# One query projection as two units of their own, and a layer norm in two stages ordered by hand

## The chip, the cores and the metric

The kernel runs on 1 core of one Trainium2 chip. The metric is the device time of one execution in microseconds (us), less is better. The engines are named as the profile names them: PE (TensorE matmul), PEld (its weight load), DVE (VectorE), ACT (ScalarE), POOL (GpSimd), SP (SyncE, which only issues transfers here).

## The reference, cut to what matters

```python
x = A_x                                     # (1, 2048, 640), bf16
xn = layernorm(x)
q = (xn @ wq)                               # 32 heads of 192
p = softmax(q k^T / sqrt(192))              # keys and values: 2048 per head
s = (p v) @ wo
g = silu( (silu(xn @ w1) * (xn @ w3)) @ w2 )
return x + s * g
```

Most of the time goes to scores and values of the 32 heads: the last projection, the one for head 31, ends 1825 us into the 2169, and the scores and values of head 31 are still to come. The query projection of a head has 192 columns: 128, and 64 more. The 64 more share a 128-column matmul with 64 columns of w1 or w3, so each head and query block needs two matmul groups of five: one with `wqB` (64 columns of w1 or w3, and 64 of the query) and one with `wq` (the first 128 of the query).

## The kernel before

The kernel's matmuls write to PSUM tiles: one ring of three of 1024 fp32 columns (`ps_st`, tag `st2`), which scores, projections, transposes and the output all use in turn, and one tile (`obank`) for the values. A unit of work is one head and one block of 512 queries: two score groups of four score tiles, each followed by a group of value matmuls, and then the projection of the same block for the next head.

```python
def project(h, qb):
    ...
    ps = ps_st.tile([P, 1024], F32, tag="st2", name="ps")
    for c in range(DC):                                      # line 288: first half
        nc.tensor.matmul(ps[:, 512:1024], lhsT=L["wqB"][:, c, :], rhs=xnT[:, c, qs], ...)
    nc.scalar.copy(out=qAB[:, 1, qs], in_=ps[:, 512:1024])   # line 289
    for c in range(DC):                                      # line 291: second half
        nc.tensor.matmul(ps[:, 0:512], lhsT=L["wq"][:, c, 0:P], rhs=xnT[:, c, qs], ...)
    nc.vector.tensor_copy(out=qAB[:, 0, qs], in_=ps[:, 0:512])
    nc.gpsimd.dma_start(out=qC[0:64, :, qs], in_=qAB[64:P, :, qs])
    nc.gpsimd.dma_start(out=qC[64:P, 0, qs], in_=qAB[0:64, 0, qs])

# scores of one tile read KA, KB, KC (keys) and qAB, qC (queries);
# KC and qC are copies on other partitions, made by DMA from POOL's queue

load_x(0); load_w(0); load_k(0)            # load_k also issues the KC copies
...
load_w(1); load_k(1); load_v(1)            # (cut) loads of head 1
...
layer_norm(0)                              # statistics, rstd on POOL, xn, transposes
project(0, 0)
pending = emit_scores(*stream[0][:3])
layer_norm(1)
project(0, 1)
for n, (h, qb, pairs, first, last) in enumerate(stream):
    pts = pending
    if n + 1 < len(stream):
        pending = emit_scores(*stream[n + 1][:3])
    ...                                    # values of group n into obank
    if h == 0 and first and qb + 2 < NQB:
        layer_norm(qb + 2)
        project(0, qb + 2)
    if not last:
        continue
    ...                                    # DVE: reciprocal, scaling of obank into ostage
    if h + 1 < H:
        project(h + 1, qb)
    ...
```

The traces show the instructions of each engine in the order of this program (in the kernel before, POOL's `rstd` at 33.91 us stands behind the key copies at 31.26 and 33.35). The program names no waits between engines; the framework puts them in.

Of the kernel before, what the change touches and what calls it, by code (L numbers as in the profile page):

```python
# [9 lines left out]
ALU = mybir.AluOpType  # L10
AX = mybir.AxisListType
BF16 = mybir.dt.bfloat16
F32 = mybir.dt.float32
I32 = mybir.dt.int32

P = 128
# [76 lines left out]
def _output_stage(nc, i, oT, g, wo_sb, x2, out2, sb, ps_pool):  # L93

    D = out2.shape[1]
    OC = wo_sb.shape[1]
    xt = sb.tile([P, D], BF16, tag="xt", name="xt")
    nc.gpsimd.dma_start(out=xt[:], in_=x2[i * P:(i + 1) * P, :])
    ps = ps_pool.tile([P, 1024], F32, tag="st2", name="ps_s")
    for k in range(OC):  # L100
        for b, (c0, c1) in enumerate(_column_pieces(D)):
            nc.tensor.matmul(ps[:, b * 512:b * 512 + c1 - c0], lhsT=oT[:, k, :], rhs=wo_sb[:, k, c0:c1],  # L102
                             start=(k == 0), stop=(k == OC - 1))
    tmp = sb.tile([P, D], F32, tag="tmp", name="tmp")
    res = sb.tile([P, D], BF16, tag="res", name="res")
    for b, (c0, c1) in enumerate(_column_pieces(D)):
        nc.vector.scalar_tensor_tensor(out=tmp[:, c0:c1].rearrange("p (a w) -> p a w", w=P),  # L107
                                       in0=ps[:, b * 512:b * 512 + c1 - c0].rearrange("p (a w) -> p a w", w=P),
                                       scalar=0.5, in1=g[:, c0 // P:c1 // P, :], op0=ALU.mult, op1=ALU.mult)
        nc.vector.tensor_tensor(out=res[:, c0:c1], in0=tmp[:, c0:c1], in1=xt[:, c0:c1], op=ALU.add)  # L110
    nc.scalar.dma_start(out=out2[i * P:(i + 1) * P, :], in_=res[:])
# [9 lines left out]
def _kernel_impl(  # L121
# [95 lines left out]
    def load_k(h):  # L217
        kh = A_k_cache[0, h]
        KA = kvp.tile([P, SK], BF16, tag="KA", name="KA")
        nc.sync.dma_start_transpose(out=KA[:], in_=kh[:, 0:P])  # L220
        KB = kvp.tile([P, SK], BF16, tag="KB", name="KB")
        nc.sync.dma_start_transpose(out=KB[:], in_=kh[:, DH - P:DH])  # L222
        KC = kvp.tile([P, HK], BF16, tag="KC", name="KC")
        nc.gpsimd.dma_start(out=KC[64:P, :], in_=KA[0:64, HK:SK])
        nc.gpsimd.dma_start(out=KC[0:64, :], in_=KB[64:P, 0:HK])
        loads.setdefault(h, {}).update(KA=KA, KB=KB, KC=KC)

    def load_v(h):
        vt = vts[h % 2]
        nc.sync.dma_start(out=vt[:, :, 0:DH], in_=A_v_cache[0, h].rearrange("(t p) d -> p t d", p=P))  # L230
        loads.setdefault(h, {}).update(vt=vt)

    load_x(0)
    load_w(0)
    load_k(0)
    for g in range(1, NQB):
        load_x(g)
    load_v(0)
    load_w(1)
    load_k(1)  # L240
    load_v(1)
    mhalf = const.tile([P, 4], F32, name="mhalf")
    nc.vector.memset(mhalf[:], -0.5)
    for vt in vts:
# [4 lines left out]
    while D // nsub > nc.vector.BN_STATS_FMAX or D % nsub != 0:  # L249
        nsub += 1  # L250

    def layer_norm(g):
        mv = lnp.tile([P, 4, nc.vector.BN_AGGR_DIM], F32, tag="mv", name="mv")
        for i in range(4):
            stats = lnp.tile([P, nsub, nc.vector.BN_STATS_DIM], F32, tag="stats", name="stats")
            xr = x_sb[:, 4 * g + i, :].rearrange("p (a f) -> p a f", a=nsub)
            for a in range(nsub):
                nc.vector.bn_stats(out=stats[:, a, :], in_=xr[:, a, :])  # L258
            nc.vector.bn_aggr(out=mv[:, i, :], in_=stats[:])
        ve = lnp.tile([P, 4], F32, tag="ve", name="ve")  # L260
        nc.vector.tensor_scalar(out=ve[:], in0=mv[:, :, 1], scalar1=eps, scalar2=None, op0=ALU.add)
        rstd = lnp.tile([P, 4], F32, tag="rstd", name="rstd")
        nc.gpsimd.tensor_tensor(out=rstd[:], in0=ve[:], in1=mhalf[:], op=ALU.pow)  # L263
        for i2 in range(2):
            pst = ps_st.tile([P, 2, DC, P], BF16, tag="st2", name="pst")
            for k in range(2):
                i = 2 * i2 + k
                xn = lnp.tile([P, D], BF16, tag="xn", name="xn")
                nc.vector.tensor_scalar(out=xn[:], in0=x_sb[:, 4 * g + i, :], scalar1=mv[:, i, 0:1], scalar2=rstd[:, i:i + 1],  # L269
                                        op0=ALU.subtract, op1=ALU.mult)  # L270
                for c in range(DC):
                    nc.tensor.transpose(out=pst[:, k, c, :], in_=xn[:, c * P:(c + 1) * P], identity=ident_bf[:])  # L272
            q0 = (4 * g + 2 * i2) * P
            nc.scalar.copy(out=xnT[:, :, q0:q0 + 2 * P].rearrange("p c (k q) -> p k c q", k=2), in_=pst[:])  # L274
# [1 line left out]

    qtiles = {}

    def project(h, qb):

        L = loads[h]
        if qb == 0:
            qtiles[h] = (qp.tile([P, 2, SQ], BF16, tag="qAB", name="qAB"), qlp.tile([P, 2, SQ], BF16, tag="qC", name="qC"))
        qAB, qC = qtiles[h]
        qs = slice(qb * 512, (qb + 1) * 512)
        ps = ps_st.tile([P, 1024], F32, tag="st2", name="ps")
        for c in range(DC):
            nc.tensor.matmul(ps[:, 512:1024], lhsT=L["wqB"][:, c, :], rhs=xnT[:, c, qs], start=(c == 0), stop=(c == DC - 1))  # L288
        nc.scalar.copy(out=qAB[:, 1, qs], in_=ps[:, 512:1024])  # L289
        for c in range(DC):  # L290
            nc.tensor.matmul(ps[:, 0:512], lhsT=L["wq"][:, c, 0:P], rhs=xnT[:, c, qs], start=(c == 0), stop=(c == DC - 1))  # L291
        nc.vector.tensor_copy(out=qAB[:, 0, qs], in_=ps[:, 0:512])  # L292
        nc.gpsimd.dma_start(out=qC[0:64, :, qs], in_=qAB[64:P, :, qs])  # L293
        nc.gpsimd.dma_start(out=qC[64:P, 0, qs], in_=qAB[0:64, 0, qs])  # L294

    def swiglu(h, qb):

# [42 lines left out]
            pts.append(pT2)  # L340
        return pts

    layer_norm(0)
    project(0, 0)
    pending = emit_scores(*stream[0][:3])
    layer_norm(1)
    project(0, 1)
    obank = None
    ostage = None
    w_all = None  # L350
    for n, (h, qb, pairs, first, last) in enumerate(stream):
        if first and qb == 0:
            if h == H // 2:
                w_all = fw.tile([P, WX], BF16, tag="xw", name="w_all")
                w2_sb = w_all[:, 0:FC * D].rearrange("p (c d) -> p c d", d=D)
                nc.sync.dma_start(out=w2_sb, in_=B_w2.rearrange("(c p) d -> p c d", p=P))
                w1_sb = w3_sb = None
                if FL > 0:
                    o1 = FC * D
                    w1_sb = w_all[:, o1:o1 + DC * FL].rearrange("p (c f) -> p c f", f=FL)  # L360
                    w3_sb = w_all[:, o1 + DC * FL:o1 + 2 * DC * FL].rearrange("p (c f) -> p c f", f=FL)
                    nc.sync.dma_start(out=w1_sb, in_=B_w1[:, FPIG:F].rearrange("(c p) f -> p c f", p=P))
                    nc.sync.dma_start(out=w3_sb, in_=B_w3[:, FPIG:F].rearrange("(c p) f -> p c f", p=P))
            if h % HG == 0:
                ostage = stp.tile([P, NQT, HG * DH], BF16, tag="ostage", name="ostage")
        pts = pending
        if n + 1 < len(stream):
            pending = emit_scores(*stream[n + 1][:3])
        if first:
            obank = ps_o.tile([P, 1024], F32, tag="ob", name="obank")  # L370
        vt = loads[h]["vt"]
        for p, pT2 in zip(pairs, pts):
            for t in range(2):
                for j in range(4):
                    start = p == 0 and t == 0 and j % 2 == 0
# [1 line left out]
                    nc.tensor.matmul(obank[:, j * 256:j * 256 + DH + 1],  # L377
                                     lhsT=pT2[:, t * 512 + j * P:t * 512 + (j + 1) * P],
                                     rhs=vt[:, t * NPAIR + p, 0:DH + 1], start=start, stop=stop)
        if h == 0 and first and qb + 2 < NQB:  # L380
            layer_norm(qb + 2)
            project(0, qb + 2)
        if not last:
            continue
        hg = h % HG
        ov = obank[:].rearrange("p (j w) -> p j w", j=4)
        rl = rl_all[:, h * NQT + qb * 4:h * NQT + qb * 4 + 4]
        nc.vector.reciprocal(out=rl, in_=ov[:, :, DH])  # L388
        nc.vector.tensor_tensor(out=ostage[:, qb * 4:qb * 4 + 4, hg * DH:(hg + 1) * DH], in0=ov[:, :, 0:DH],  # L389
                                in1=rl.unsqueeze(2).to_broadcast([P, 4, DH]), op=ALU.mult)  # L390
        if h + 1 < H:
            project(h + 1, qb)
        if h < 2 * NPIG:
            swiglu(h, qb)
        if qb == 1 and h + 2 < H:
            load_w(h + 2)
        if qb == NQB - 1:
            if h + 2 < H:
                load_k(h + 2)
                load_v(h + 2)  # L400
            del loads[h]
            if hg == HG - 1:
                g0 = h - hg
                nc.sync.dma_start(
                    out=o_scr.rearrange("(t p) c -> p t c", p=P)[:, :, g0 * DH:(g0 + HG) * DH],
                    in_=ostage[:, :, :],
                )
    att.close()


# [3 lines left out]
    wo_sb = wop.tile([P, OC, D], BF16, name="wo_sb")  # L414
    nc.gpsimd.dma_start(out=wo_sb[:], in_=A_wo.rearrange("(k p) d -> p k d", p=P))
    oTs = {}

    def load_oT(i, pool):
        if i < NQT:
# [118 lines left out]
```

## Time and profile before

| | before |
|---|---|
| time, median (range), 3 runs | 2171.22 us (2167.99 to 2171.72) |
| span of the profiled run | 2168.7 us |
| PE / ACT / DVE / POOL busy | 94% / 51% / 19% / 13% |
| one unit (head and query block) | 14.07 us |
| first PE instruction | 35.49 us |

The first part of the page of the kernel before gives busy time, share of the span and number of instructions of each engine.

```profile
PE 2027.9 (94%) x17777; PEld 1285.7 (59%) x17777; DVE 408.2 (19%) x718; ACT 1108.7 (51%) x1273; POOL 277.8 (13%) x443
```

PE is the engine that sets the time. It is idle for 2168.7 - 2027.9 = 140.8 us, and the view of PE's waits (line and tile that waited, engine and line that ended the wait, us in total, times, longest) of the kernel before says where:

```profile
PE ps L291 <- ACT qAB L289: 86.1, 128, 0.7
PE pst L272 <- DVE xn L269: 39.2, 6, 35.5
PE ps L288 <- ACT xnT L274: 6.1, 4, 1.9
PE st_215 L336 <- DMA qC<-qAB: 2.1, 1, 2.1
...
```

Line 291, the second half of the projection, waits in all 128 units for ACT's copy of the first half. The timeline of the kernel before shows one such wait (start, duration, engine, line, operation, output<-input, in brackets the idle time before it and what ended it):

```profile
1006.29 1.24 PE L288 MATMUL ps<-xnT,wqB 128*128 128x512 bf16 x5
1006.49 0.18 DVE L388 RECIPROCAL rl_all<-obank 128x4 f32<-128x4 f32 x1 [9.75 <-PE obank L377]
1006.70 0.96 DVE L389 TENSOR_TENSOR ostage<-obank,rl_all 128x768 bf16<-128x768 f32 x1
1007.57 0.58 ACT L289 CAST qAB<-ps 128x512 bf16<-128x512 f32 x1 [2.02 <-PE ps L288]
1008.20 1.24 PE L291 MATMUL ps<-xnT,wq 128*128 128x512 bf16 x5 [0.67 <-ACT qAB L289]
1009.37 0.39 PE L336 MATMUL st_11021<-qAB,KA 64*128 64x512 bf16 x1
```

The two halves start 1.91 us apart. Five matmuls of 512 columns took 1.08 us from start to start where nothing held them (0.216 us each). The true hole is therefore 1.91 - 1.08 = 0.83 us; the brackets say 0.67, because the matmuls before are counted as busy for 1.24 us, until the modelled end of the last. 128 such holes are 106 us.

The start has the other large hole. This is the timeline of its first 36 us in the kernel before:

```profile
9.31 0.17 DVE L261 TENSOR_SCALAR ve<-mv 128x4 f32<-128x4 f32 x1
...
31.26 0.58 POOL L224 DMA_DIRECT2D KC<-KA  x1 [13.11 <-DMA KA<-in_A_k_cache_dram]
33.35 0.54 POOL L225 DMA_DIRECT2D KC<-KB  x1 [1.51 <-DMA KB<-in_A_k_cache_dram]
33.91 1.05 POOL L263 TENSOR_TENSOR rstd<-ve,mhalf 128x4 f32<-128x4 f32 x1
34.99 0.80 DVE L269 TENSOR_SCALAR xn<-x_all,mv,rstd 128x640 bf16<-128x640 bf16 x2 [25.51 <-POOL rstd L263]
```

The variance is ready at 9.5 us, but POOL computes `rstd` only at 33.9 us, because the key copies of head 1 stand before it in POOL's queue and wait for loads. PE starts 0.5 us after `xn` has begun.

### The profile page before, as it was taken

The page shows a single profiled execution, that of the slowest core. Times are in us where ns is not written, and L with a number is a line of the kernel's source. Part 1 is how long each engine was busy: PE and PEld are TensorE (multiplying, and loading weights), DVE is VectorE, ACT ScalarE, POOL GpSimd, SP SyncE. Part 2 cuts the span into 40 slices and gives each one's busy share as a digit, 9 for nine tenths or more (in the row PEclk, how much of TensorE's full clock was granted, in tenths as well). Part 3 has the DMA queues.
Part 4 walks back from the last instruction along what each step waited for, and adds up shares of the span by engine and source line. Part 5 has one row for each costly group of instructions (what it writes and reads, how often), then busy time and mean ns, then how long its engine had stood idle before and what let it go on. Part 6 is the DMA issues. An engine that isn't in the chain of part 4 may idle for free.

```text
span 2168.7 us, 39997 instructions
## 1 busy us (share of the span) xinstructions
PE 2027.9 (94%) x17777; PEld 1285.7 (59%) x17777; DVE 408.2 (19%) x718; ACT 1108.7 (51%) x1273; POOL 277.8 (13%) x443
## 2 busy tenths in 40 slices
PE   2799999999999999999999999999999999999998
PEld 1465565666555566656556665655665566577776
DVE  2311111111111111111111111111111111431111
ACT  1465556565656565655655665565566556420000
POOL 2111111111111111111111111111111110000000
PEclk9899999999999999999999999999999999999999
DMA  7023232323333232325232333232323230565773
GB/s 144 16 62 91 62 91 61 88 62 91 62 90 62 64 77 52 90 59 145 55 85 60 91 62 91 59 89 57 91 63 91 62 91 12 133 136 106 144 152 71
DMA packets 359731, 177.38 MB, mean 82 GB/s; under 512 B 305536, under 2 KB 346240, under 8 KB 359552
## 3 DMA queue, kind: packets, MB, share of 16 engines
q1 hardware_dynamic: 335984, 114.96, 24.3%
q0 software_dynamic: 21264, 57.18, 10.8%
q8 instruction: 141, 2.31, 0.4%
q10 hardware_dynamic: 2304, 2.62, 0.4%
q14 instruction: 38, 0.31, 0.0%
HBM read 54.66 MB, written 27.79 MB: 38 GB/s over the span
## 4 chain that ended last, share of the span: by engine, by line
PE 93%; ACT 4%; SPq 1%; DVE 1%; issue 1%; DMA 0%; POOL 0%; POOLq 0%; DVEq 0%
PE obank L377 32%; PE ps_s L102 10%; PE ps L291 7%; PE ps L288 7%; ACT qAB L289 4%; PE ps_f L459 2%; PE ps_gu L433 1%; PE ps_gu L430 1%; SPq L220 1%; ACT xnT L274 0%; SPq L222 0%; DVE stats L258 0%; DMA KB<-in_A_k_cache_dram 0%; PE pst L272 0%; POOL rstd L263 0%
## 5 line engine op out<-in xcount | busy, mean ns | idle before, releaser
L293 POOL DMA_DIRECT2D qC<-qAB x128 | 78.4, 613 | 1517.8 <-DVE qAB L292 1517.8
L388 DVE RECIPROCAL rl_all<-obank 128x4 f32<-128x4 f32 x128 | 23.4, 183 | 1225.0 <-PE obank L377 1225.0
L291 PE MATMUL ps<-xnT,wq 128*128 128x512 bf16 x640 | 161.8, 384 | 86.1 <-ACT qAB L289 86.1
L102 PE MATMUL ps_s<-wo_sb,oT 128*128 128x384 bf16 (+1 forms) x1536 | 208.8, 300 | 0.0
L289 ACT CAST qAB<-ps 128x512 bf16<-128x512 f32 x128 | 74.9, 585 | 258.9 <-PE ps L288 258.9
L336 PEld LDWEIGHTS <-KA 64*128 64x128 bf16 x1024 | 96.3, 94 | 167.6 <-issue 77.7
L102 PEld LDWEIGHTS <-oT 128*128 128x128 bf16 x1536 | 149.9, 98 | 58.6
L291 PEld LDWEIGHTS <-wq 128*128 128x128 bf16 x640 | 62.5, 98 | 185.5 <-issue 126.1
L288 PE MATMUL ps<-xnT,wqB 128*128 128x512 bf16 x640 | 162.2, 385 | 6.1 <-ACT xnT L274 6.1
L336 PEld LDWEIGHTS <-KC 64*128 64x128 bf16 x1024 | 96.2, 94 | 118.4 <-issue 1.6
L292 DVE CAST qAB<-ps 128x512 bf16<-128x512 f32 x128 | 88.5, 692 | 261.5 <-PE ps L291 261.5
L336 PEld LDWEIGHTS <-KB 64*128 64x128 bf16 x1024 | 96.8, 94 | 61.4 <-issue 1.4
L389 DVE TENSOR_TENSOR ostage<-obank,rl_all 128x768 bf16<-128x768 f32 x128 | 122.5, 957 | 4.4
L337 PEld LDWEIGHTS <-KA 64*128 64x128 bf16 x1024 | 96.1, 94 | 45.4 <-issue 43.5
L337 PEld LDWEIGHTS <-KB 64*128 64x128 bf16 x1024 | 97.7, 95 | 2.6 <-issue 2.6
L337 PEld LDWEIGHTS <-KC 64*128 64x128 bf16 x1024 | 96.9, 95 | 0.0
L288 PEld LDWEIGHTS <-wqB 128*128 128x128 bf16 x640 | 61.2, 98 | 53.4 <-issue 9.1
L294 POOL DMA_DIRECT2D qC<-qAB x128 | 67.8, 530 | 0.2 <-issue 0.2
L459 PE MATMUL ps_f<-w_all,hT 128*128 128x384 bf16 (+1 forms) x384 | 52.3, 300 | 0.0
L107 DVE SCALAR_TENSOR_TENSOR tmp<-ps_s,hT 128x384 f32<-128x384 f32 (+1 forms) x32 | 15.6, 487 | 177.4 <-PE ps_s L102 177.4
L459 PEld LDWEIGHTS <-hT 128*128 128x128 bf16 x384 | 37.5, 98 | 14.8
L272 PE MATMUL pst<-ident_bf,xn 128*128 128x128 bf16 x80 | 7.3, 244 | 39.2 <-DVE xn L269 39.2
(9262 smaller groups left out, 5352.2 us busy)
## 6 DMA issues: line engine op xcount, KB each, us to landing
o_scr<-ostage SPq DMA_DIRECT2D x16, 1536.0 KB, 8.3
qC<-qAB POOLq DMA_DIRECT2D x128, 128.0 KB, 2.3
vt_109<-in_A_v_cache_dram SPq DMA_DIRECT2D x16, 768.0 KB, 5.1
vt_110<-in_A_v_cache_dram SPq DMA_DIRECT2D x16, 768.0 KB, 5.2
qC<-qAB POOLq DMA_DIRECT2D x128, 64.0 KB, 2.0
wq<-in_A_wq_dram POOLq DMA_DIRECT2D x32, 240.0 KB, 3.6
wo_sb<-in_A_wo_dram POOLq DMA_DIRECT2D x1, 7680.0 KB, 39.0
KC<-KA POOLq DMA_DIRECT2D x32, 128.0 KB, 5.3
```

The lines of the kernel that those rows point to most:

```text
L102: nc.tensor.matmul(ps[:, b * 512:b * 512 + c1 - c0], lhsT=oT[:, k, :], rhs=wo_sb[:, k, c0:c1], start=(k == 0), stop=(k == OC - 1))
L288: nc.tensor.matmul(ps[:, 512:1024], lhsT=L["wqB"][:, c, :], rhs=xnT[:, c, qs], start=(c == 0), stop=(c == DC - 1))
L289: nc.scalar.copy(out=qAB[:, 1, qs], in_=ps[:, 512:1024])
L291: nc.tensor.matmul(ps[:, 0:512], lhsT=L["wq"][:, c, 0:P], rhs=xnT[:, c, qs], start=(c == 0), stop=(c == DC - 1))
L292: nc.vector.tensor_copy(out=qAB[:, 0, qs], in_=ps[:, 0:512])
L293: nc.gpsimd.dma_start(out=qC[0:64, :, qs], in_=qAB[64:P, :, qs])
L294: nc.gpsimd.dma_start(out=qC[64:P, 0, qs], in_=qAB[0:64, 0, qs])
L336: nc.tensor.matmul(st2[:, 0:512], lhsT=k0, rhs=q0, start=r == 0, stop=r == 2)
L337: nc.tensor.matmul(st2[:, 512:1024], lhsT=k1, rhs=q1, start=r == 0, stop=r == 2)
L377: nc.tensor.matmul(obank[:, j * 256:j * 256 + DH + 1], lhsT=pT2[:, t * 512 + j * P:t * 512 + (j + 1) * P], rhs=vt[:, t * NPAIR + p, 0:DH + ...
L389: nc.vector.tensor_tensor(out=ostage[:, qb * 4:qb * 4 + 4, hg * DH:(hg + 1) * DH], in0=ov[:, :, 0:DH], in1=rl.unsqueeze(2).to_broadcast([P ...
L459: nc.tensor.matmul(ps[:, b * 512:b * 512 + c1 - c0], lhsT=hT[:, fc, i * P:(i + 1) * P], rhs=w2_sb[:, fc, c0:c1], start=(fc == 0), stop=(fc ...
```

## The change

Its intent: each half of a projection becomes a unit with a ring tile of its own, copied by DVE, and one half stands behind each of the two score groups of a unit; the layer norm is cut into statistics (`ln_stats`) and normalisation with transposes (`ln_norm`), and both, with the key copies (`copy_k`) and the loads, are put in an order by hand. The output loop takes one column piece after the other. The diff, cut to its core:

```diff
-    for k in range(OC):
-        for b, (c0, c1) in enumerate(_column_pieces(D)):
+    for b, (c0, c1) in enumerate(_column_pieces(D)):
+        for k in range(OC):
             nc.tensor.matmul(ps[:, b * 512:b * 512 + c1 - c0], lhsT=oT[:, k, :], rhs=wo_sb[:, k, c0:c1], ...
 ... (KC copies out of load_k into copy_k; layer_norm split; rstd for two row tiles at a time)
-    def project(h, qb):
+    def project(h, qb, half):
 ...
         ps = ps_st.tile([P, 1024], F32, tag="st2", name="ps")
         for c in range(DC):
-            nc.tensor.matmul(ps[:, 512:1024], lhsT=L["wqB"][:, c, :], rhs=xnT[:, c, qs], ...
-        nc.scalar.copy(out=qAB[:, 1, qs], in_=ps[:, 512:1024])
-        for c in range(DC):
-            nc.tensor.matmul(ps[:, 0:512], lhsT=L["wq"][:, c, 0:P], rhs=xnT[:, c, qs], ...
-        nc.vector.tensor_copy(out=qAB[:, 0, qs], in_=ps[:, 0:512])
-        nc.gpsimd.dma_start(out=qC[0:64, :, qs], in_=qAB[64:P, :, qs])
-        nc.gpsimd.dma_start(out=qC[64:P, 0, qs], in_=qAB[0:64, 0, qs])
+            w = L["wqB"][:, c, :] if half else L["wq"][:, c, 0:P]
+            nc.tensor.matmul(ps[:, 0:512], lhsT=w, rhs=xnT[:, c, qs], ...
+        nc.vector.tensor_copy(out=qAB[:, half, qs], in_=ps[:, 0:512])
+        nc.gpsimd.dma_start(out=qC[0:64, half, qs], in_=qAB[64:P, half, qs])
+        if half == 0:
+            nc.gpsimd.dma_start(out=qC[64:P, 0, qs], in_=qAB[0:64, 0, qs])
 ...
+    load_x(0)
+    load_w(0)
+    load_k(0)
+    ln_stats(0)
+    load_x(1)
+    load_v(0)
+    ...
+    ln_norm(0)
+    project(0, 0, 1)
+    project(0, 0, 0)
+    copy_k(0)
+    ln_stats(1)
+    scores(0)
+    load_w(1)
+    load_k(1)
+    load_v(1)
+    for n, (h, qb, pairs, first, last) in enumerate(stream):
+        if h == 0 and last and qb + 1 < NQB:
+            values(n)
+            project(0, qb + 1, 1)
+            project(0, qb + 1, 0)
+            if qb + 2 < NQB:
+                ln_stats(qb + 2)
+            scores(n + 1)
+        else:
+            if n + 1 < len(stream):
+                scores(n + 1)
+            values(n)
+            if h == 0 and first and qb + 1 < NQB:
+                ln_norm(qb + 1)
+        if first and h + 1 < H and h > 0:
+            project(h + 1, qb, 1)
+        if last:
+            if h + 1 < H:
+                ...
+                project(h + 1, qb, 0)
```

More of the change, by code (lines that the diff above doesn't have):

```diff
@@ L222, in load_k, with copy_k @@
         nc.sync.dma_start_transpose(out=KB[:], in_=kh[:, DH - P:DH])
+        loads.setdefault(h, {}).update(KA=KA, KB=KB)
+    def copy_k(h):
+        KA, KB = loads[h]["KA"], loads[h]["KB"]
         KC = kvp.tile([P, HK], BF16, tag="KC", name="KC")
@@ L225, in load_k @@
         nc.gpsimd.dma_start(out=KC[0:64, :], in_=KB[64:P, 0:HK])
-        loads.setdefault(h, {}).update(KA=KA, KB=KB, KC=KC)
+        loads[h].update(KC=KC)
     def load_v(h):
@@ L231, in load_v @@
         loads.setdefault(h, {}).update(vt=vt)
-    load_x(0)
-    load_w(0)
-    load_k(0)
-    for g in range(1, NQB):
-        load_x(g)
-    load_v(0)
-    load_w(1)
-    load_k(1)
-    load_v(1)
     mhalf = const.tile([P, 4], F32, name="mhalf")
@@ L250, in _kernel_impl, with ln_stats @@
         nsub += 1
-    def layer_norm(g):
+    lnorm = {}
+    def ln_stats(g):
         mv = lnp.tile([P, 4, nc.vector.BN_AGGR_DIM], F32, tag="mv", name="mv")
+        ve = lnp.tile([P, 4], F32, tag="ve", name="ve")
+        rstd = lnp.tile([P, 4], F32, tag="rstd", name="rstd")
         for i in range(4):
@@ L259, in layer_norm, with ln_norm @@
             nc.vector.bn_aggr(out=mv[:, i, :], in_=stats[:])
-        ve = lnp.tile([P, 4], F32, tag="ve", name="ve")
-        nc.vector.tensor_scalar(out=ve[:], in0=mv[:, :, 1], scalar1=eps, scalar2=None, op0=ALU.add)
-        rstd = lnp.tile([P, 4], F32, tag="rstd", name="rstd")
-        nc.gpsimd.tensor_tensor(out=rstd[:], in0=ve[:], in1=mhalf[:], op=ALU.pow)
+            if i % 2 == 1:
+                two = slice(i - 1, i + 1)
+                nc.vector.tensor_scalar(out=ve[:, two], in0=mv[:, two, 1], scalar1=eps, scalar2=None, op0=ALU.add)
+                nc.gpsimd.tensor_tensor(out=rstd[:, two], in0=ve[:, two], in1=mhalf[:, two], op=ALU.pow)
+        lnorm[g] = (mv, rstd)
+    def ln_norm(g):
+        mv, rstd = lnorm[g]
         for i2 in range(2):
@@ L277, in _kernel_impl @@
     qtiles = {}
-    def project(h, qb):
+    def project(h, qb, half):
         L = loads[h]
-        if qb == 0:
+        if h not in qtiles:
             qtiles[h] = (qp.tile([P, 2, SQ], BF16, tag="qAB", name="qAB"), qlp.tile([P, 2, SQ], BF16, tag="qC", name="qC"))
@@ L287, in project @@
         for c in range(DC):
-            nc.tensor.matmul(ps[:, 512:1024], lhsT=L["wqB"][:, c, :], rhs=xnT[:, c, qs], start=(c == 0), stop=(c == DC - 1))
-        nc.scalar.copy(out=qAB[:, 1, qs], in_=ps[:, 512:1024])
-        for c in range(DC):
-            nc.tensor.matmul(ps[:, 0:512], lhsT=L["wq"][:, c, 0:P], rhs=xnT[:, c, qs], start=(c == 0), stop=(c == DC - 1))
-        nc.vector.tensor_copy(out=qAB[:, 0, qs], in_=ps[:, 0:512])
-        nc.gpsimd.dma_start(out=qC[0:64, :, qs], in_=qAB[64:P, :, qs])
-        nc.gpsimd.dma_start(out=qC[64:P, 0, qs], in_=qAB[0:64, 0, qs])
+            w = L["wqB"][:, c, :] if half else L["wq"][:, c, 0:P]
+            nc.tensor.matmul(ps[:, 0:512], lhsT=w, rhs=xnT[:, c, qs], start=(c == 0), stop=(c == DC - 1))
+        nc.vector.tensor_copy(out=qAB[:, half, qs], in_=ps[:, 0:512])
+        nc.gpsimd.dma_start(out=qC[0:64, half, qs], in_=qAB[64:P, half, qs])
+        if half == 0:
+            nc.gpsimd.dma_start(out=qC[64:P, 0, qs], in_=qAB[0:64, 0, qs])
     def swiglu(h, qb):
@@ L341, in emit_scores, with scores, values @@
         return pts
-    layer_norm(0)
-    project(0, 0)
-    pending = emit_scores(*stream[0][:3])
-    layer_norm(1)
-    project(0, 1)
-    obank = None
-    ostage = None
-    w_all = None
-    for n, (h, qb, pairs, first, last) in enumerate(stream):
-        if first and qb == 0:
-            if h == H // 2:
-                w_all = fw.tile([P, WX], BF16, tag="xw", name="w_all")
-                w2_sb = w_all[:, 0:FC * D].rearrange("p (c d) -> p c d", d=D)
-                nc.sync.dma_start(out=w2_sb, in_=B_w2.rearrange("(c p) d -> p c d", p=P))
-                w1_sb = w3_sb = None
-                if FL > 0:
-                    o1 = FC * D
-                    w1_sb = w_all[:, o1:o1 + DC * FL].rearrange("p (c f) -> p c f", f=FL)
-                    w3_sb = w_all[:, o1 + DC * FL:o1 + 2 * DC * FL].rearrange("p (c f) -> p c f", f=FL)
-                    nc.sync.dma_start(out=w1_sb, in_=B_w1[:, FPIG:F].rearrange("(c p) f -> p c f", p=P))
-                    nc.sync.dma_start(out=w3_sb, in_=B_w3[:, FPIG:F].rearrange("(c p) f -> p c f", p=P))
-            if h % HG == 0:
-                ostage = stp.tile([P, NQT, HG * DH], BF16, tag="ostage", name="ostage")
-        pts = pending
-        if n + 1 < len(stream):
-            pending = emit_scores(*stream[n + 1][:3])
+    exps = {}
+    obanks = {}
+    ostages = {}
+    wrest = {}
+    def scores(n):
+        exps[n] = emit_scores(*stream[n][:3])
+    def values(n):
+        h, qb, pairs, first, last = stream[n]
         if first:
-            obank = ps_o.tile([P, 1024], F32, tag="ob", name="obank")
+            obanks[0] = ps_o.tile([P, 1024], F32, tag="ob", name="obank")
+        obank = obanks[0]
         vt = loads[h]["vt"]
-        for p, pT2 in zip(pairs, pts):
+        for p, pT2 in zip(pairs, exps.pop(n)):
             for t in range(2):
@@ L379, in _kernel_impl @@
                                      rhs=vt[:, t * NPAIR + p, 0:DH + 1], start=start, stop=stop)
-        if h == 0 and first and qb + 2 < NQB:
-            layer_norm(qb + 2)
-            project(0, qb + 2)
         if not last:
-            continue
+            return
         hg = h % HG
+        if hg == 0 and qb == 0:
+            ostages[0] = stp.tile([P, NQT, HG * DH], BF16, tag="ostage", name="ostage")
+        ostage = ostages[0]
         ov = obank[:].rearrange("p (j w) -> p j w", j=4)
@@ L390, in _kernel_impl, with loads_after @@
                                 in1=rl.unsqueeze(2).to_broadcast([P, 4, DH]), op=ALU.mult)
-        if h + 1 < H:
-            project(h + 1, qb)
-        if h < 2 * NPIG:
-            swiglu(h, qb)
+    def loads_after(h, qb):
         if qb == 1 and h + 2 < H:
             load_w(h + 2)
+        if qb == 1 and h == H // 2:
+            w_all = fw.tile([P, WX], BF16, tag="xw", name="w_all")
+            wrest["w2"] = w_all[:, 0:FC * D].rearrange("p (c d) -> p c d", d=D)
+            nc.sync.dma_start(out=wrest["w2"], in_=B_w2.rearrange("(c p) d -> p c d", p=P))
+            if FL > 0:
+                o1 = FC * D
+                for i, (nm, src) in enumerate((("w1", B_w1), ("w3", B_w3))):
+                    wrest[nm] = w_all[:, o1 + i * DC * FL:o1 + (i + 1) * DC * FL].rearrange("p (c f) -> p c f", f=FL)
+                    nc.sync.dma_start(out=wrest[nm], in_=src[:, FPIG:F].rearrange("(c p) f -> p c f", p=P))
         if qb == NQB - 1:
@@ L400, in _kernel_impl @@
                 load_v(h + 2)
+                copy_k(h + 2)
             del loads[h]
-            if hg == HG - 1:
-                g0 = h - hg
+            if h % HG == HG - 1:
+                g0 = h - HG + 1
                 nc.sync.dma_start(
                     out=o_scr.rearrange("(t p) c -> p t c", p=P)[:, :, g0 * DH:(g0 + HG) * DH],
-                    in_=ostage[:, :, :],
+                    in_=ostages[0][:, :, :],
                 )
+    load_x(0)
[4 more added lines that the diff above has]
+    load_v(0)
+    for g in range(2, NQB):
+        load_x(g)
+    ln_norm(0)
[25 more added lines that the diff above has]
+            if h + 1 < H:
+                if h == 0:
+                    project(1, qb, 1)
+                    if qb == 0:
+                        copy_k(1)
+                project(h + 1, qb, 0)
+            if h < 2 * NPIG:
+                swiglu(h, qb)
+            loads_after(h, qb)
     att.close()
@@ L416, in _kernel_impl @@
     oTs = {}
+    w2_sb, w1_sb, w3_sb = wrest["w2"], wrest.get("w1"), wrest.get("w3")
     def load_oT(i, pool):
```

## The prediction

> **What bounds the kernel now.** TensorE. The page gives PE 94% busy (2027.9 of 2168.7 us), ACT 51%, DVE 19%; the chain that ended last is 93% PE. PE is idle for 141 us, and the view of waits names nearly all of it: 86.1 us in 128 waits of 0.67 us, where the second half of the projection (L291) waits for ACT's copy of the first half (L289); 39.2 us for the layer norm's xn, 35.5 of them once at the start.
>
> **The steady unit** (timeline, one head and query block): 14.07 us. The two projection halves start 1.91 us apart, and five matmuls stream in 1.08 us. So the true hole is 0.83 us, not 0.67 (ends are modelled): the second half writes other columns of a tile that ACT is still reading.
>
> **What the change does there.** Each half gets its own tile of the ring of three and its copy goes to DVE: 10 ring tiles a unit, not 9; the same matmuls. The wait disappears unless it comes back at the third score tile after a half, which now waits for DVE's copy. Behind the first group: copy ends 0.28 + 0.69 = 0.97 us after the half, the tile is wanted 0.09 + 1.29 = 1.38 us after it. Behind the second group DVE first finishes reciprocal and scaling (1.37 us after the values end), so the copy ends about 2.1 us after the values, wanted at 2.46. Both fit, with 0.3 to 0.4 us to spare. DVE gains 128 x 0.69 us, ACT loses 128 x 0.585; neither is critical. 120 projections outside head 0 give 120 x 0.83 = 100 us.
>
> **Start.** Before, rstd on POOL is queued behind the K copies of head 1 (waits for KB until 33.3 us) although the variance was ready at 9.5; PE starts at 35.5. After, rstd stands ahead: PE should start near 10 us, projection near 14. Then a new hole: the K copies stand behind the query copies, so the first score tile waits for qC and KC until about 27 us (estimate: issue at 21, plus the 6 us such copies take here). Before: 48.1.
> New cost in head 0: for query blocks 1 to 3 projection and scores are back to back, so scores wait for copy and DMA (0.97 + 0.8 + 2.0, less one round): about 3.4 us each. [...] Stepped through, head 0 ends near 112 us against 137: 25 us gained.
>
> **End.** The output loop's new order has the same matmuls; DVE still waits for the whole tile, so nothing.
>
> **Sum.** 2171 - 100 - 25 = 2046 us. 80% range 2034 to 2066.
> Faster by over 2%: 0.96; within 2%: 0.035; slower: 0.005.
>
> **What would show it.** PE busy 98% or more; no L291 wait on L289, none as large on DVE's qAB copy; unit 13.2 us; first PE instruction near 10 us; three waits of 2 to 4 us on qC in head 0.
>
> **What would make it wrong.** DVE's copy late at the third score tile (each 0.1 us costs 13 us, at both places 25); first loads slower in the new order; a lower clock in the denser run.

One sentence is cut from the paragraph on the start: it added time in each of query blocks 1 to 3 for matmuls at a lower clock, by a rule that no trace shows. The sums stand with that term in them: 25 us gained in head 0, and 2046 us in all. So the terms that are left do not make up the 25 us by themselves; without the term the forecast would have been a few us lower. What the trace before does show: the five matmuls at 68.97 us took 2.29 us, at a granted clock of 0.50 (68.97 to 71.27 us), where the five at 1006.29 us took 1.24 us at 1.00 (1000 to 1010 us).

## The result, and the profile after

| | before | after |
|---|---|---|
| time, median (range) | 2169.60 us (2167.32 to 2171.72), 4 runs | 2049.01 us (2045.92 to 2051.03), 4 runs |
| ratio | | 0.9443 (95% interval 0.9426 to 0.9461) |
| span of the profiled run | 2168.7 us | 2046.2 us |
| one unit | 14.07 us | 13.24 us |
| first PE instruction | 35.49 us | 10.14 us |

The runs before are those of the first table and one more. A ratio is the mean time of one kernel's fast runs over that of the other's of the same rounds, so it is not quite the ratio of the medians in the table.

The same line of the page, of the kernel after:

```profile
PE 1991.1 (97%) x17529; PEld 1282.7 (63%) x17777; DVE 485.7 (24%) x850; ACT 1031.5 (50%) x1145; POOL 337.0 (16%) x575
```

PE's busy time fell by 36.8 us, although the matmuls are the same. Two things make the difference. First, 248 records are missing from this trace (17529 of 17777): e6 and e7 below run the same matmuls, have all 17777 records and show PE busy for 2004.8 us (98%), so the missing ones take some 14 us. e6's line:

```profile
PE 2004.8 (98%) x17777; PEld 1283.1 (63%) x17777; DVE 485.6 (24%) x850; ACT 1031.4 (50%) x1145; POOL 335.9 (16%) x575
```

Second, each removed hole also removes a modelled matmul end that had been counted as busy: 128 x (0.83 - 0.67) is about 20 us of the other 23 (an estimate). PE's waits in the kernel after:

```profile
PE pst L275 <- DVE xn L272: 11.1, 4, 10.1
PE st_229 L338 <- DMA qC<-qAB: 7.9, 1, 7.9
PE st_900 L338 <- DMA qC<-qAB: 4.9, 1, 4.9
PE st_229 L338 <- DMA KC<-KB: 2.3, 1, 2.3
PE st_451 L338 <- DMA qC<-qAB: 1.8, 1, 1.8
PE st_687 L338 <- DMA qC<-qAB: 1.8, 1, 1.8
...
```

The 128 waits of the projection are gone and no other wait has taken their place; what is left lies in head 0. One steady half unit in the timeline of the kernel after (PE, DVE, and the starts of the first and the third score tile behind the half):

```profile
1011.94 1.24 PE L292 MATMUL ps<-xnT,wq 128*128 128x512 bf16 x4
...
1012.36 0.96 DVE L376 TENSOR_TENSOR ostage<-obank,rl_all 128x768 bf16<-128x768 f32 x1
1013.12 0.39 PE L338 MATMUL st_12139<-qAB,KA 64*128 64x512 bf16 x1
1013.23 0.68 DVE L293 CAST qAB<-ps 128x512 bf16<-128x512 f32 x1
...
1014.42 0.38 PE L338 MATMUL st_12157<-qAB,KA 64*128 64x512 bf16 x1
```

The half streams in 1.18 us to the first score tile with no hole. DVE's copy is done at 1013.91 us; the third score tile, which gets the half's ring tile, starts 0.51 us later and on time.

The start in the timeline of the kernel after answers to the one of before:

```profile
9.57 0.17 DVE L261 TENSOR_SCALAR ve<-mv 128x2 f32<-128x2 f32 x1
9.64 0.80 DVE L272 TENSOR_SCALAR xn<-x_all,mv,rstd 128x640 bf16<-128x640 bf16 x2
9.81 0.82 POOL L262 TENSOR_TENSOR rstd<-ve,mhalf 128x2 f32<-128x2 f32 x1 [1.49 <-DVE ve L261]
...
19.05 0.54 POOL L294 DMA_DIRECT2D qC<-qAB  x1 [1.12 <-DVE qAB L293]
...
20.61 0.52 POOL L229 DMA_DIRECT2D KC<-KB  x1
...
27.07 0.58 PE L338 MATMUL st_229<-qC,KB 64*128 64x512 bf16 x1 [7.88 <-DMA qC<-qAB]
30.03 0.61 PE L338 MATMUL st_229<-qC,KC 64*128 64x512 bf16 x1 [2.34 <-DMA KC<-KB]
```

`rstd` of the second pair of row tiles follows its variance at once. A new hole opens: the query copy asked for at 19.05 us is there only at 27.07, and the key copy asked for at 20.61 only at 30.03. The second of these moments varies between traces of the same start: in e3, e5, e6 and e7 the last round of the first score tile starts between 26.68 and 31.42 us.

Where the 122.5 us between the two spans lie can be read from the starts of the projections. The second half for head 1, block 3 starts at 136.15 us before and at 111.35 after: 24.8 us by the end of head 0. From there to the last projection matmul (1824.9 before, 1701.6 after) it is 120 units: 123.3 - 24.8 = 98.5 us, or 0.82 us a unit. From there to the end of the span: 343.8 before, 344.6 after.

### The profile page after: what moved, and what is told of

The parts are those of the page before. It is cut to its first block, busy times and chain, and to the rows that moved or that the text cites. A ratio compares the mean times of both kernels' runs of the same rounds, so it can differ in the third digit from the quotient of the medians.

```text
span 2046.2 us, 39879 instructions
## 1 busy us (share of the span) xinstructions
PE 1991.1 (97%) x17529; PEld 1282.7 (63%) x17777; DVE 485.7 (24%) x850; ACT 1031.5 (50%) x1145; POOL 337.0 (16%) x575
## 4 chain that ended last, share of the span: by engine, by line
PE 97%; DMA 1%; issue 1%; DVE 1%; ACT 0%; POOL 0%; DVEq 0%; ACTq 0%; POOLq 0%
PE obank L364 35%; PE ps L292 13%; PE ps_s L102 10%; PE ps_f L503 3%; PE ps_gu L477 1%; PE ps_gu L474 1%; DMA KC<-KB 0%; DMA qC<-qAB 0%; PE pst L275 0%; DMA x_all<-in_A_x_dram 0%; DVE stats L257 0%; DVE xn L272 0%; DVE qAB L293 0%; PE st_238 L338 0%; PE st_256 L338 0%
## 5 line engine op out<-in xcount | busy, mean ns | idle before, releaser
L294 POOL DMA_DIRECT2D qC<-qAB x256 | 136.5, 533 | 1343.9 <-DVE qAB L293 1343.9
L293 DVE CAST qAB<-ps 128x512 bf16<-128x512 f32 x256 | 175.7, 686 | 654.2 <-PE ps L292 654.2
L102 PE MATMUL ps_s<-wo_sb,oT 128*128 128x256 bf16 (+1 forms) x1536 | 208.8, 299 | 0.0
L292 PE MATMUL ps<-xnT,wqB 128*128 128x512 bf16 x516 | 153.5, 381 | 8.0 <-ACT xnT L277 1.3
L292 PE MATMUL ps<-xnT,wq 128*128 128x512 bf16 x520 | 153.4, 381 | 6.3
L339 PEld LDWEIGHTS <-KB 64*128 64x128 bf16 x1024 | 97.4, 95 | 17.9 <-issue 17.5
L296 POOL DMA_DIRECT2D qC<-qAB x128 | 67.1, 525 | 0.2 <-issue 0.2
L98 POOL DMA_DIRECT2D xt<-in_A_x_dram x16 | 8.6, 540 | 253.2 <-DVE res L110 253.2
L308 DVE SCALAR_TENSOR_TENSOR hT<-pt,qAB 64x512 bf16<-64x512 bf16 x64 | 43.5, 679 | 1.0
```

Of the source, the lines that this page charges most:

```text
L102: nc.tensor.matmul(ps[:, b * 512:b * 512 + c1 - c0], lhsT=oT[:, k, :], rhs=wo_sb[:, k, c0:c1], start=(k == 0), stop=(k == OC - 1))
L292: nc.tensor.matmul(ps[:, 0:512], lhsT=w, rhs=xnT[:, c, qs], start=(c == 0), stop=(c == DC - 1))
L293: nc.vector.tensor_copy(out=qAB[:, half, qs], in_=ps[:, 0:512])
L294: nc.gpsimd.dma_start(out=qC[0:64, half, qs], in_=qAB[64:P, half, qs])
L308: nc.vector.scalar_tensor_tensor(out=hid, in0=t[:], scalar=1.0, in1=z, op0=ALU.add, op1=ALU.mult)
L339: nc.tensor.matmul(st2[:, 512:1024], lhsT=k1, rhs=q1, start=r == 0, stop=r == 2)
```

## The experiments

All kernels gave correct results. The first four ran on one chip, the next six on another, each beside runs of the kernel before on the same chip (medians 2170.84 and 2168.64 to 2168.74 us). So a difference of a few us between two experiments is read from the ratios, or from the traces, and not from the medians alone.

### e1: only the tile of the first half

```diff
-        ps = ps_st.tile([P, 1024], F32, tag="st2", name="ps")
+        psB = ps_st.tile([P, 1024], F32, tag="st2", name="psB")
         for c in range(DC):
-            nc.tensor.matmul(ps[:, 512:1024], lhsT=L["wqB"][:, c, :], ...
-        nc.scalar.copy(out=qAB[:, 1, qs], in_=ps[:, 512:1024])
+            nc.tensor.matmul(psB[:, 0:512], lhsT=L["wqB"][:, c, :], ...
+        nc.scalar.copy(out=qAB[:, 1, qs], in_=psB[:, 0:512])
+        ps = ps_st.tile([P, 1024], F32, tag="st2", name="ps")
```

(on the kernel before)

> The kernel before with one edit: the first half of the projection writes a tile of its own (one more tile of the ring of three), still copied by ACT, both halves still behind the last score group. My theory: the whole steady gain is the second half's wait for the first half's copy out of a shared tile, 0.83 us in each of 128 projections, so 2170 - 107 = 2063 us (2057 to 2070), no wait of the second half on ACT's copy, unit of 13.24 us, start unchanged (first PE work at 35.5 us). Rival (the halves must be parted and put behind different groups, or the copy must leave ACT): the time stays above 2120 us because the wait turns up again as a wait for a free tile.

Measured: 2061.30 us (2056.67 to 2062.83), ratio to before 0.9491 (0.9471 to 0.9511). In e1's timeline the second half follows the first without a hole, while ACT still copies the first:

```profile
1012.58 1.24 PE L288 MATMUL psB<-xnT,wqB 128*128 128x512 bf16 x5
...
1013.66 1.24 PE L292 MATMUL ps<-xnT,wq 128*128 128x512 bf16 x5
1013.86 0.58 ACT L289 CAST qAB<-psB 128x512 bf16<-128x512 f32 x1 [2.02 <-PE psB L288]
```

The halves start 1.08 us apart instead of 1.91. Three lines of the change carry 109.5 of its 120.6 us. The wait was the shared tile's, not ACT's: ACT still copies, and PE no longer waits for it. Whether the hardware needed the wait inside the shared tile is not shown, for no run here lets PE write one half of it while ACT reads the other. In e1, PE writes one tile from 1013.66 on while ACT reads another until 1014.44, with correct results.

### e2: the old projection in the new order of the start

On the kernel after: `project` as before (one tile, ACT and DVE copies, both halves behind the last group), everything else as after.

> The kernel after with only the projection put back: both halves in one tile, back to back behind the last group, ACT copies the first and DVE the second, two query copies by DMA as before; the new order of the start stays. It measures the start alone. My theory: 128 waits of 0.83 us come back, 2049 + 107 = 2156 us (2150 to 2163), that is, the start alone is worth 14 us or so (25 less the 6.6 us of waits in head 0, less what holes of head 0 I undersized). Rival (the gains are not additive, the start hides part of it): outside that range.

Measured: 2157.13 us (2156.59 to 2160.59), ratio to before 0.9943 (0.9925 to 0.9960). The view of waits has the old line back:

```profile
PE ps L296 <- ACT qAB L294: 86.6, 128, 1.1
```

The start alone gives 13.7 us by the medians; the interval lies below 1, but the gain is under 2%. In its trace the second half for head 1, block 3 starts at 119.88 us, 16.3 us earlier than before. Alone, the two parts give 109.5 + 13.7 = 123.2 us, together 120.6, and the runs of one kernel spread over 4 to 8 us: within that, the parts add up.

### e3: own tiles, but both halves behind the last group

```diff
-        if first and h + 1 < H and h > 0:
-            project(h + 1, qb, 1)
         if last:
             if h + 1 < H:
-                if h == 0:
-                    project(1, qb, 1)
-                    if qb == 0:
-                        copy_k(1)
+                project(h + 1, qb, 1)
+                if h == 0 and qb == 0:
+                    copy_k(1)
                 project(h + 1, qb, 0)
```

> The kernel after, own tiles and DVE copies kept, but both halves again together behind the last group instead of one behind each. My theory: the placement is worth nothing, since neither the ring nor DVE is short: 2049 us within 5. Rival (the spreading carries the gain, because two projection tiles in a row leave the ring of three short for the next scores): 2060 us or more, with waits of the second or third score tile for DVE's copy.

Measured: 2051.19 us (2048.86 to 2051.99), ratio to before 0.9447 (0.9431 to 0.9462), against 0.9443 for the change. The placement, the part that gives the change its name, is worth nothing that can be measured here. The separate tiles are enough.

### e4: the copy done twice

```diff
         nc.vector.tensor_copy(out=qAB[:, half, qs], in_=ps[:, 0:512])
+        nc.vector.tensor_copy(out=qAB[:, half, qs], in_=ps[:, 0:512])
```

> The kernel after with each of DVE's 256 copies out of PSUM done twice (same data, same place). It measures the slack of that copy, which the prediction put at 0.3 to 0.4 us; the trace after shows 0.51 us (copy done at 1007.28, third score tile started at 1007.79). A second copy adds 0.65 to 0.7 us, so 0.15 to 0.2 us becomes a wait at each of 248 halves: 37 to 50 us more, 2086 to 2099 us, as waits of the third score tile for DVE. If the slack is as I predicted: 70 to 90 us more. If the copy isn't what frees the third tile: no change.

Measured: 2104.23 us (2103.75 to 2105.31), that is 55 us over the change; more than the 37 to 50 that I expected, less than the 70 to 90 that the prediction's slack of 0.3 to 0.4 us would give. In e4's timeline:

```profile
1006.02 0.39 PE L339 MATMUL st<-qAB,KA 64*128 64x512 bf16 x1
1006.14 0.68 DVE L293 CAST qAB<-ps 128x512 bf16<-128x512 f32 x1
...
1006.86 0.69 DVE L294 CAST qAB<-ps 128x512 bf16<-128x512 f32 x1
...
1007.60 0.37 PE L339 MATMUL st<-qAB,KA 64*128 64x512 bf16 x1
```

The third score tile starts 1.58 us after the first, against 1.30 in the kernel after (1013.12 to 1014.42), so it is 0.28 us late. The second copy begins 0.72 us after the first, so the slack had been 0.72 - 0.28 = 0.44 us. A half unit takes 6.84 us (1006.02 to 1012.86 in the trace) instead of 6.62: 0.22 x 248 = 55 us. Note that no bracket stands behind the late line, and that the view of waits of e4 has only 5 us more than that of the kernel after: 0.28 us shows up as hardly any idle time when the matmul before it is counted as busy until its modelled end. Short waits of PE have to be read from the distance of starts.

### e5: ACT copies the first half again

```diff
-        nc.vector.tensor_copy(out=qAB[:, half, qs], in_=ps[:, 0:512])
+        if half == 1:
+            nc.scalar.copy(out=qAB[:, 1, qs], in_=ps[:, 0:512])
+        else:
+            nc.vector.tensor_copy(out=qAB[:, 0, qs], in_=ps[:, 0:512])
```

> The kernel after, with the copy of the first half (the one behind the first score group) on ACT again, DVE keeps the other. My theory: moving the copy from ACT to DVE is worth nothing, ACT is free for more than 2 us there: 2049 us within 4. Rival (ACT needs the relief because the copy delays the next exponentials): 5 us or more slower, with more waits of score tiles for exponentials.

Measured: 2048.11 us (2046.50 to 2050.71), ratio to before 0.9446 (0.9433 to 0.9459). The engine of this copy does not matter.

### e6: the output loop put back

Chunk outside and column piece inside, as before the change.

> The kernel after with the loop of the output projection put back (chunk outside, column piece inside). Same matmuls, DVE waits for the whole tile either way: 2049 us within 3, last matmul to end of span unchanged at about 7 us. Rival (the new order lets DVE start on the first piece early): about 1 us slower per run, tail longer by that.

Measured: 2049.86 us (2045.54 to 2051.65), ratio to before 0.9452 (0.9439 to 0.9465). No difference that these runs can tell; an effect of 1 us either way would be hidden in the spread. In the kernel after, DVE still reads the last tile's first piece only at 2038.96 us, behind the start of the tile's last matmul at 2038.7 us. In the traces, the time from the start of the last output matmul to the end of the span is 6.9 us in e6, and 7.5 and 6.8 us in the kernel after and in e7, which both have the new order.

### e7: a weight load of head 0 one block later

```diff
-        if qb == 1 and h + 2 < H:
+        if qb == (2 if h == 0 else 1) and h + 2 < H:
             load_w(h + 2)
```

In the timeline of the kernel after, the query copies of head 0's last block (block 3) were issued late:

```profile
87.18 0.69 DVE L293 CAST qAB<-ps 128x512 bf16<-128x512 f32 x1 [0.39 <-PE ps L292]
87.44 0.91 POOL L205 DMA_DIRECT2D wq<-in_A_wq_dram  x1 [10.20 <-PE ps L292]
...
90.06 1.12 POOL L294 DMA_DIRECT2D qC<-qAB  x2
...
93.19 0.58 PE L338 MATMUL st_900<-qC,KB 64*128 64x512 bf16 x1 [4.88 <-DMA qC<-qAB]
```

POOL had stood at the weight load for 10.2 us, because the tile of the weights became free only with the projection just before; three issues of 0.9 us each then came ahead of the query copies.

> The kernel after, but in head 0 the weights of head 2 are asked for one query block later. In the trace after, the third query copy of head 0 was issued only at 90.1 us, 2.2 us after its data were ready, because POOL stood at that weight load (its tile was free only after the projection just before), so PE waited 4.9 us there instead of the 1.8 us of the other two blocks, and then ran at half clock for 2.5 us. My theory: that wait goes to 1.8 us and the half clock stretch with it: 4 us faster, 2045 us (2042 to 2047). Rival (DMA congestion, not POOL's queue): no change.

Measured: 2044.75 us (2041.19 to 2048.41), ratio to before 0.9434 (0.9421 to 0.9447). The median is 4.3 us below that of the change, as expected, but the intervals of the two ratios overlap; the trace decides. In it the wait of block 3 has become the same as for the other blocks:

```profile
87.92 0.37 PE L338 MATMUL st<-qC,KB 64*128 64x512 bf16 x1 [1.78 <-DMA qC<-qAB]
```

From block 3's projection to the next projection it is 8.2 us (82.64 to 90.88), where the kernel after has 12.2 (84.82 to 97.02) and e6, which still loads early, 12.1 (83.26 to 95.33). So POOL's queue made that wait, and 4 us is what it cost.

### e8 and e9: what the first query copy waits for

e8 is e7 with `copy_k(0)` ahead of the projection and with the loads of head 1 held back on SP by a tiny transfer that reads the query copy; e9 also holds back V of head 0 and the last two blocks of x.

```diff
     ln_norm(0)
+    copy_k(0)
     project(0, 0, 1)
     project(0, 0, 0)
-    copy_k(0)
     ln_stats(1)
+    nc.sync.dma_start(out=gate[:], in_=qtiles[0][1][64:65, 0, 0:64])
+    # e9: load_v(0), load_x(2), load_x(3) here instead of ahead of ln_norm(0)
     scores(0)
```

> As e7, and also the K copies of head 0 ahead of the query copies on POOL, and the loads of head 1 held back on SP (by a tiny transfer that reads the query copy) until the query copies of head 0 have landed. It tests the largest hole left at the start: 7.9 us for the query copy and 2.3 us for KC in the first score tile (landing 8 us after issue, while the loads of head 1 run). My theory: the copy is slow because it shares the DMA engines with those loads; alone it lands in 2 to 3 us, so 6 to 8 us less beyond e7: 2038 us (2035 to 2042), first exponential near 23 to 25 us instead of 30.7. Rival (the copies would be slow anyway, or what is held back is missed later): less than 3 us beyond e7.

> As e8, but the held-back loads now include V of head 0 and the last two blocks of x, so that nothing but K of head 0 and one block of x is in flight when the query copies go. In e8 the query copy still took 6.5 us from issue to use (18.72 to 25.20), since those loads were still running. My theory (contention on the DMA engines): it lands 2 to 3 us after issue, the second round of the first score tile starts near 21.5 us instead of 25.2, 3 to 4 us less than e8: 2037 us (2034 to 2039). Rival (the copies are slow at the start for another reason, or V of head 0 now comes too late for the first values): no better than e8, 2040 us, or worse.

Measured: e8 2040.53 us (2039.71 to 2042.24), ratio to before 0.9413 (0.9400 to 0.9425); e9 2040.18 us (2038.81 to 2042.27), ratio 0.9410 (0.9398 to 0.9422). The DMA views of the window from 10 to 30 us give the median time from issue to landing of the three query copies. In the kernel after:

```profile
qC<-qAB POOLq DMA_DIRECT2D x3, 64.0 KB, 8.0
```

In e8:

```profile
qC<-qAB POOLq DMA_DIRECT2D x3, 64.0 KB, 6.4
```

In e9:

```profile
qC<-qAB POOLq DMA_DIRECT2D x3, 64.0 KB, 1.9
```

e8 is 4.2 us under e7 by the medians, between the 6 to 8 that I expected and the rival's 3. The copy did not land in 2 to 3 us, and the first exponential starts at 26.39 us, not at 23 to 25. Its 6.4 us is no sure gain on the 8.0 either: in e3, e5, e6 and e7, which start as the kernel after does, the same view gives 6.7, 10.6, 7.8 and 5.6. e9's 1.9 is far outside all of them, and it differs from e8 only in the loads held back. So the copy was slow because of what else was in flight. The DMA rows of the two views agree: from 17.5 to 23 us, with the copies asked for from 17.3 us on in e8 and 17.4 in e9, the 16 DMA engines were busy 90% or more in e8 and under 50% in e9. The copies are issued by POOL and the loads beside them by SP.

Yet e9 is no faster than e8. Its first scores do start early, and the projection of block 1 starts at 34.84 us against 40.01 in e8, 5.2 us ahead. The held-back loads now run while block 1's query copy goes (from 34 to 46 us its DMA view gives 4.8 us to landing, e8's 1.9), and in e9's timeline PE waits there instead, with score matmuls of 0.58 to 0.63 us behind it, where those of block 3 in the same run take 0.37 to 0.39:

```profile
43.01 0.58 PE L339 MATMUL st<-qC,KB 64*128 64x512 bf16 x1 [4.67 <-DMA qC<-qAB]
```

In e8 that wait was 1.76 us. The next projection of head 1 starts at 47.72 us in e9 and 48.23 in e8. The rival expectation for e9 (2040 us) came true, for neither of the reasons it gave: the wait was moved by one block, not taken away.

### e10: transposes in the hole

e9, and in head 0 the normalisation and transposes of the next block stand between a block's projection and its scores, where PE waits for the query copies. The diff shows the loop; `ln_norm(1)` and `ln_stats(2)` also move ahead of `scores(0)`, and the old call of `ln_norm` in the loop goes.

```diff
             project(0, qb + 1, 1)
             project(0, qb + 1, 0)
             if qb + 2 < NQB:
-                ln_stats(qb + 2)
+                ln_norm(qb + 2)
+            if qb + 3 < NQB:
+                ln_stats(qb + 3)
             scores(n + 1)
```

> As e9, and in head 0 the transposes of the layer norm of the next query block but one are put between the block's own projection and its scores, where PE otherwise waits 2.6 us for the query copies. The waits fall on work that has to be done anyway (1.65 us of transposes a block, 4 blocks, with 0.3 us of their own waits): 4 to 8 us less than e9, 2031 us (2028 to 2034). Rival (the score tiles then wait for ACT's copy of the transposes in the ring of three): less than 2 us gained.

Measured: 2036.81 us (2035.46 to 2037.71), ratio to before 0.9391 (0.9378 to 0.9404): 3.4 us under e9 by the medians, short of the 4 to 8 I expected and over the rival's 2. The waits for the query copies fell from 9.9 us in e9 to 1.8 us, but those for `xn` rose from 11.2 to 18.7, as e10's view of waits shows:

```profile
PE pst L276 <- DVE xn L273: 18.7, 6, 10.2
PE st L339 <- DMA qC<-qAB: 1.8, 1, 1.8
```

In program order DVE first copies the projection and then makes `xn`, so the transposes start late in the hole (in block 1, PE waits 1.14 us for `xn` after the projection) and only part of it is filled. Behind block 0's projection the hole even grew: there DVE also makes the statistics of block 1 first, and PE waits 5.59 us for `xn`, where in e9 it waited 0.78 us for DVE's copy and 1.73 us for the query copy. e10 is the fastest kernel, 12 us (0.6%) under the change by the medians.

## Why the prediction was right

- **Bound by PE, one large hole a unit.** Right. The hole was sized by the distance of starts (0.83 us) and not by the idle time of the profile (0.67 us). The steady gain measured 98.5 us over 120 units, predicted 100; the idle figure alone would have given 80. The granted clock, a risk that the prediction named, was 0.996 before and 0.995 after. The sign "PE busy 98% or more" reads 97% in the trace after, which lacks 248 records, and 98% in e6 and e7, which lack none.
- **The wait does not come back at the third score tile.** Right. The slack was predicted at 0.3 to 0.4 us; e4 measured 0.44. DVE's copies grew by 87 us (88.5 to 175.7), as predicted (128 x 0.69), and e5 shows that the move of the first half's copy from ACT is neutral.
- **Start, first PE instruction near 10 us.** Right (10.14 us), as `rstd` no longer stands behind the key copies.
- **Head 0 gains 25 us.** The sum was right (24.8 us), but partly by luck: its terms have errors that cancel, and the start differs from run to run. The moment that stands at 111.35 us in the kernel after (second half for head 1, block 3) is at 112.89 in e5 and 109.66 in e6, which do nothing else in head 0 that should move it, so the gain lies between 23 and 27 us. The first score tile was predicted to be complete about 27 us and its last round began at 30.03: I took 6 us for the copies under load, and they took 8.0 and 9.4. The holes of blocks 1 to 3 were put at 3.4 us each and were 0.8 + 1.8 = 2.6 us in blocks 1 and 2. Block 3 had 0.8 + 4.9 us, from a weight load in POOL's queue that I had not seen (e7). The cut term stood for a lower clock behind each of the three waits; in the trace after, the granted clock was 0.50 only behind block 3's (93.19 to 95.70 us) and at the first scores (27.0 to 34.2 us), and 1.00 behind those of blocks 1 and 2 (49.5 to 52.1 and 69.7 to 72.4 us). So the sign "three waits of 2 to 4 us on qC" did not come as told: they were 1.8, 1.8 and 4.9 us.
- **A lower clock behind the waits.** Shown in part. In the trace after, behind the 4.88 us wait, score matmuls take 0.58 to 0.63 us instead of 0.38, at the granted clock of 0.50. But the length of one wait does not decide it. The gaps in the trace before were, after the start, short: ahead of the projection at 68.97 us, whose five matmuls took 2.29 us, PE had waited 1.26, 0.19 and 1.44 us around its transposes. In e7, behind a shorter wait of 1.74 us in block 2, they were slow too:

```profile
64.52 0.37 PE L338 MATMUL st<-qAB,KA 64*128 64x512 bf16 x1 [0.78 <-DVE qAB L293]
66.65 0.58 PE L338 MATMUL st<-qC,KB 64*128 64x512 bf16 x1 [1.74 <-DMA qC<-qAB]
```

  while behind the wait of 1.78 us in block 3 of the same run they were not (0.37 us). No run here shows what sets it; the cause of the slow matmuls behind the short waits stays open.
- **Output loop: nothing.** e6 finds no difference, within its spread of some 3 us either way.

What was not foreseen is how little of the change was needed. The prediction costed the spreading and the new engine as neutral, and e3 and e5 show that they are; it did not say that a tile for the first half would give nine tenths of the gain, which e1 shows.

## What to carry to other kernels

When an engine waits for a reader of another part of the same tile, give each part a tile of its own before anything is moved: here that alone gave 109.5 of the 120.6 us (e1). Size a hole of PE by the distance of starts less the streaming time, not by the idle time of the profile (here 0.83 us against 0.67), and compare the copy that frees a buffer with the moment it is next wanted. When loads are shifted to speed up one small copy, ask which copy they will meet next: e9 only moved the wait (in block 1, 4.67 us in place of e8's 1.76).
